# A transformer block on one Trainium2 core: the low halves of the feed-forward weights made by an adding transfer, with the sequence of all steps searched anew

## The chip, the cores and the metric

The kernel runs on one core of a Trainium2 chip. A core has five engines with an instruction queue each: PE (TensorE, matmuls), ACT (ScalarE), DVE (VectorE), POOL (GpSimd) and SP (SyncE, which here only issues transfers); 16 DMA engines move data between the core's SBUF and the chip's memory. An engine takes its instructions strictly in the order in which they were written, so an instruction that waits holds up everything behind it on its engine. The metric is the device time of one execution in microseconds (us); less is better.

## What is computed

The reference is one transformer layer in float32: S = 2048 tokens of width 640, 32 heads of width 20, an attention in which each token looks at 8 earlier tokens, two apart, and a gated feed-forward part (SwiGLU) of width 1728.

```python
def _layernorm(x, axis=-1, eps=1e-5):
    ...
B, S, D = 1, 2048, 640                         # F = 1728
def _A_ref(x, wqkv, wo):
    qkv = (x @ wqkv).reshape(B, S, 3, H, Dh)   # H = 32, Dh = 20
    ...
    off = jnp.arange(W) * dil                  # W = 8, dil = 2
    idx = pos[:, None] - off[None, :]
    ...
    logits = jnp.einsum("bhsd,bhswd->bhsw", q, kg) * scale
    logits = jnp.where(mask[None, None, :, :], logits, -1e9)
    attn = _softmax(logits, axis=-1)
    o = jnp.einsum("bhsw,bhswd->bhsd", attn, vg)
    return o.reshape(B, S, D) @ wo
def _B_ref(x, w_gate, w_up, w_down):
    g = _silu(x @ w_gate)
    u = x @ w_up
    return (g * u) @ w_down
h = x + _A_ref(_layernorm(x), A_wqkv, A_wo)
h2 = h + _B_ref(_layernorm(h), B_w_gate, B_w_up, B_w_down)
return h2
```

## The kernel before

**Numbers in halves.** TensorE multiplies here in a rounded 32-bit form (fp32r). To keep the accuracy of float32, every operand is held as two halves: the high half is the rounded value, the low half is the raw value minus the high half, rounded again. Each product is then made in three passes into the same accumulator (one PSUM bank): high times high, high times low, low times high. A high half of a weight is a copy by ACT that rounds; a low half is a subtraction by DVE (`split`, 640 columns at a time, line L956).

**Tiling.** The tokens are worked on in four blocks of 512, b = 0 to 3, and the feed-forward weights in NF = 14 column blocks, i = 0 to 13 (the last is half as wide and comes from an array of its own). Stages: layernorm and QKV projection (matmuls L643, results taken from the bank by ACT L648) for all blocks; attention on DVE, with the exponential on ACT (`att_qk` L692 and L699, `att_exp` L710 to L712, `att_av` L721 to L735, a little of it on POOL); the output projection `wo` (matmuls L890, copied out by ACT L893, added to the residual by DVE L896); a second layernorm; the feed-forward part. Between a layernorm and its matmuls the normalised tokens are turned into columns: `pair_columns` (L490 ff.) makes their halves in the tile `shb`, by ACT L495 and L506 and DVE L496 and L507. `shb` is also what the QKV matmuls read, so the columns of the first feed-forward block overwrite what the last QKV matmuls read.

**Feed-forward part.** Blocks b = 0 and b = 1 run through `ffn(b)`; b = 2 and 3 through a scheme that shares products between the two blocks. `load_ffn(b, i, ...)` brings the weights of one column block: one transfer of 960 KB of raw weights by SP (L938: 1280 columns for gate and up, 640 for down, on 128 partitions), two rounding copies by ACT (L939 with 1280 columns, L940 with 640), and three subtractions of 640 columns by DVE (L956). For b = 0 the low halves are also stored to a scratch array in memory, `lsc` (SP, L951), and b = 1 and b = 2 take them from there (L944) instead of making them. There are two raw buffers, two buffers for gate and up, three for down. Then, for column block i: three passes of five matmuls each for the gate into bank 5 and three for up into bank 6 (`proj`, L962; in the lists below bank_73 and bank_74; the others, banks 0 to 4 and 7, are bank_68 to bank_72 and bank_75); ACT takes the silu of bank 5 (`gate`, L985), which frees that bank; DVE multiplies it by bank 6 (L986), which frees bank 6; ACT rounds the product to its high half (L996), DVE makes the low half (L997); PE multiplies both with the down weights into banks 0 to 4 (`downs`, L973, three matmuls for each bank).

**What sets the order.** The program is first recorded: `P.add(engine, cost, fn, r, w, ...)` notes a step, what it reads and what it writes. `P.order()` then returns a sequence of all steps, in which each stands behind those that it depends on, and the program is written out in that sequence; so it sets the order on every engine's queue at once. Before, the sequence comes from a planner that places steps on the engines by their assumed costs in ten rounds (`listed`, `latest`), each step's planned start being moved by an entry of a table of some 300 numbers (`SHIFT`); 2846 steps are recorded. In the time that this text speaks of most, the first feed-forward block (b = 0), the attention of blocks 2 and 3, the projection `wo(1)` and its layernorm lie on DVE, ACT and PE in between.

Of the kernel before, what the change touches and what calls it, by code (L numbers as in the profile page):

```python
# [34 lines left out]
LANES, HOP = 8, 0.035  # L35
LAP = {"PE": 0.0, "ACT": 0.1, "DVE": 0.08, "POOL": 0.0, "SP": 0.0}
ROUNDS = ((1.1, 3, 3.5), (1.5, 6, 1.5), (1.4, 20, 3.5), (1.1, 6, 3.5), (1.3, 10, 3.5), (1.0, 6, 1.5), (1.0, 3, 1.5), (1.3, 3, 3.5), (1.4, 10, 2.5),)
PR = {'tp': 6, 'mx': 2, 'mh': 2, 'ml': 2, 'mld': 3, 'dt': 2.2, 'g1': 0.6, 'y1': 0.6, 'x': 0.5, 'yst': 8, 'yld': 2, 'wqd': 4, 'wqh': 0.5, 'wql': 4, 'qev': 1, 'kvs': 0.4, 'atl': 1.2, 'exp': 0.5, 'ost': 3, 'wod': 2, 'woh': 8, 'wol': 1.2, 'old': 1.5, 'fld': 4, 'lst': 6, 'wev': 1.5, 'fh': 2.2, 'fl': 8, 'ln1': 8, 't1': 1, 'wo0': 1.2, 'wo': 2.2, 'ln1t': 1.2, 'xb': 0.4, 'tr': 10, 't1t': 2.2, 'ln1d': 0.5, 'hst': 10, 'hld': 10, 'ht': 1, 'hc': 2, 'jd': 3, 'jp': 8, 'js': 4, 'jl': 0.4, 'ja': 0.5, 'jfld': 1.2, 'jfh': 4, 'jfl': 1, 'jhi': 4, 'jmu': 0.4, 'jlo': 0.9, 'jcm': 0.5, 'w3': 1, 'w3e': 8, 'w3o': 0.4, 'w3x': 8, 'w3l': 2.2, 'jy': 6}

SHIFT = {  # L40
# [34 lines left out]
}  # L75


# [1444 lines left out]
```

## Time and profile before

| what | value |
|---|---|
| time of the kernel before, three runs | 836.15 us median (835.84, 836.15, 837.64) |
| span of the profiled execution | 835.3 us |
| time of the profiled execution itself | not recorded apart from its span; the median lies 0.85 us above the span |
| PE busy | 826.3 us, 99% of the span, 4061 matmuls |
| PE weight loads (beside the matmuls) | 712.8 us, 85% |
| DVE busy | 755.7 us, 90%, 916 instructions |
| ACT busy | 421.3 us, 50%, 740 instructions |
| POOL busy | 23.1 us, 3%, 34 instructions |
| DMA | 211.08 MB moved, 253 GB/s on the mean; SP's queue 74.0% of 16 engines' span |

The page of the profile gives each engine's busy time; the views of the trace give it by stretches of time (windows), by groups of like instructions (busy us, mean ns of one, idle time before them and what ended it), by waits, and as a chain of work that ended last. Times in a trace count from the start of the span. A line number is that of the kernel's file; in the changed kernel the same lines stand 12 further down up to `load_ffn`'s rounding copies, and 18 further behind it (L962 becomes L980, L985 becomes L1003).

### The profile page before, as it was taken

Reading aid. Unit: us, or ns where it says so; the run is one execution under the profiler, and the core shown is the slowest. Engines: PE = TensorE matmul, PEld = TensorE weight load, DVE = VectorE, ACT = ScalarE, POOL = GpSimd, SP = SyncE. Lnnn points to the kernel's source line nnn. Section 1 sums busy time; section 2 is a strip of 40 time slices with the busy share of each in tenths; the row PEclk is TensorE's granted clock in tenths of the full one; section 3 lists DMA queues with packets and bytes.
Section 4 is the critical chain, followed back from the end, with each engine's and each line's share of the span. In section 5 each row is a group of like instructions: output and inputs, shape, how many; then the busy total and the mean of one; then the engine's idle time right before and its main releaser. Section 6 shows DMA issues by size and latency. Waiting matters only on the chain.

```text
span 835.3 us, 11299 instructions
## 1 busy us (share of the span) xinstructions
PE 826.3 (99%) x4061; PEld 712.8 (85%) x4061; DVE 755.7 (90%) x916; ACT 421.3 (50%) x740; POOL 23.1 (3%) x34
## 2 busy tenths in 40 slices
PE   8999999999999999999999999999999999999998
PEld 6888888889978888887888888888988888888998
DVE  7599999999999999999999999998869888777982
ACT  7856473333783435654543476565695323323440
POOL 0000000000100000001000000000000000000000
PEclk9999999999999999999999999999999999999999
DMA  8897868568679764899899758899999634457722
GB/s 274 288 348 275 267 213 283 185 207 308 186 219 343 257 197 177 326 303 349 282 313 349 271 173 315 255 288 352 352 339 320 224 115 151 124 175 258 273 99 75
DMA packets 113223, 211.08 MB, mean 253 GB/s; under 512 B 37952, under 2 KB 70400, under 8 KB 112528
## 3 DMA queue, kind: packets, MB, share of 16 engines
q1 hardware_dynamic: 112864, 209.96, 74.0%
q8 instruction: 32, 0.52, 0.2%
q10 hardware_dynamic: 304, 0.41, 0.1%
q14 instruction: 23, 0.19, 0.1%
HBM read 151.27 MB, written 59.05 MB: 252 GB/s over the span
## 4 chain that ended last, share of the span: by engine, by line
PE 84%; DVE 8%; ACT 3%; DMA 3%; issue 1%; SPq 0%; POOL 0%; DVEq 0%; ACTq 0%; POOLq 0%
PE bank L962 22%; PE bank L1046 18%; PE bank L643 15%; PE bank L973 10%; PE bank L1298 7%; PE bank L890 6%; DMA fa<-in_x_dram 2%; PE bank L1103 1%; DVE fa L692 1%; PE bank L1093 1%; DVE fa L735 1%; PE bank L1068 1%; DVE fa L727 1%; DVE fa L699 1%; ACT ra L617 1%
## 5 line engine op out<-in xcount | busy, mean ns | idle before, releaser
L962 PE MATMUL bank<-shb,ra 128*128 128x512 f32 x810 | 190.0, 390 | 1.3 <-DVE shb L507 1.3
L962 PEld LDWEIGHTS bank<-shb,ra 128*128 128x128 f32 x810 | 151.4, 188 | 32.7 <-ACT shb L506 1.5
L643 PE MATMUL bank<-ra,sha 128*128 128x480 f32 x480 | 105.2, 379 | 0.2 <-ACT ra L617 0.2
L643 PE MATMUL bank<-ra,shb 128*128 128x480 f32 x470 | 102.5, 378 | 0.0
L643 PEld LDWEIGHTS bank<-ra,sha 128*128 128x128 f32 x480 | 89.8, 188 | 14.5 <-ACT ra L617 0.6
L643 PEld LDWEIGHTS bank<-ra,shb 128*128 128x128 f32 x470 | 88.1, 188 | 13.2
L692 DVE TENSOR_TENSOR fa<-fa 128x2560 f32<-128x2560 f32 x32 | 90.2, 2820 | 0.9 <-DMA fa<-qsc 0.4
L727 DVE TENSOR_TENSOR fa<-fa 128x2560 f32<-128x2560 f32 x32 | 90.3, 2822 | 0.8
L699 DVE TENSOR_REDUCE fa<-fa 128x128 f32<-128x2560 f32 x32 | 89.9, 2810 | 0.4
L1046 PE MATMUL bank<-shb,ra 128*128 128x512 f32 x360 | 89.4, 395 | 0.6 <-DVE fa L990 0.6
L973 PE MATMUL bank<-ra,acts 128*128 128x512 f32 x328 | 80.7, 391 | 0.0
L1046 PEld LDWEIGHTS bank<-shb,ra 128*128 128x128 f32 x360 | 66.0, 188 | 16.2 <-DVE fa L1223 1.7
L735 DVE TENSOR_TENSOR fa<-fa 128x1280 f32<-128x1280 f32 (+2 forms) x70 | 76.7, 1096 | 1.3
L890 PE MATMUL bank<-ra 128*128 128x320 f32 x480 | 74.1, 310 | 0.0
L890 PEld LDWEIGHTS bank<-ra 128*128 128x128 f32 x480 | 71.7, 188 | 2.4 <-ACT fa L893 1.0
L648 ACT ACTIVATE st<-bank,fa 128x480 f32<-128x480 f32 x64 | 41.0, 656 | 64.1 <-PE bank L643 59.5
L973 PEld LDWEIGHTS bank<-ra,acts 128*128 128x128 f32 x328 | 61.1, 188 | 13.2 <-DVE acts L997 0.5
L1046 PE MATMUL bank<-ra 128*128 128x512 f32 x288 | 69.1, 390 | 0.0
L1046 PEld LDWEIGHTS bank<-ra 128*128 128x128 f32 x288 | 53.9, 188 | 11.1
L1223 DVE TENSOR_TENSOR fa<-bank,fa 128x512 f32<-128x512 f32 x60 | 41.0, 689 | 19.8 <-PE bank L1046 19.0
L939 ACT CAST ra<-fa 128x1280 fp32r<-128x1280 f32 (+1 forms) x38 | 45.6, 1207 | 22.9 <-PE bank L962 12.3
L996 ACT CAST acts<-fa 128x512 fp32r<-128x512 f32 x34 | 21.0, 620 | 48.7 <-DVE fa L986 47.0
(189 smaller groups left out, 1059.8 us busy)
## 6 DMA issues: line engine op xcount, KB each, us to landing
fa<-in_ffn_dram SPq DMA_DIRECT2D x28, 960.0 KB, 6.4
fa<-ksc SPq DMA_DIRECT2D x16, 880.0 KB, 5.4
fa<-vsc SPq DMA_DIRECT2D x16, 880.0 KB, 7.3
ra<-lsc SPq DMA_DIRECT2D x21, 640.0 KB, 5.8
ra<-lsc SPq DMA_DIRECT2D x27, 320.0 KB, 3.7
lsc<-ra SPq DMA_DIRECT2D x13, 640.0 KB, 4.6
fa<-in_ffn_dram SPq DMA_DIRECT2D x12, 640.0 KB, 4.0
ra<-tsc SPq DMA_DIRECT2D x8, 960.0 KB, 7.1
```

Of the source, the lines that this page charges most:

```text
L643: T.matmul(banks[bk][:, 0:480], l, r_(wq(g, w, c), 480), start=(p, c) == first_mm, stop=(p, c) == last_mm)
L648: P.add("ACT", act(480) + 0.06, lambda bk=bk, j=j: A.activation(stage_t()[:, so : so + 1920].rearrange("p (t j c) -> p t j c", t=3, j=NJ)[ ...
L692: P.add("DVE", dve(2560), lambda: V.tensor_tensor(f(PROD, 2560).rearrange("p (j w c) -> p j w c", j=2, w=W), window(ko, 2 * jp), f(qo + 32 ...
L699: P.add("DVE", dve(2560), lambda: V.tensor_reduce(f(lo + 128 * jp, 128), f(PROD, 2560).rearrange("p (n d) -> p n d", d=DH), axis=AX.X, op= ...
L727: V.tensor_tensor(f(PROD, 2560).rearrange("p (j w d) -> p j w d", j=2, d=DH), bass.AP(tensor=fa[:, vo : vo + 160].tensor, offset=fa[:, vo ...
L735: V.tensor_add(dst(v), v[:, :, 0:m, :], v[:, :, m : 2 * m, :])
L890: T.matmul(banks[bk][:, 0:320], l, r_(m, 320), start=p == 0 and c == 0, stop=p == 2 and c == NC - 1)
L939: P.add("ACT", act(n), lambda: A.copy(r_(gu, n), f(raw, n)), r=[rf(raw, n)], w=[rr(gu, n)], prio=PR["fh"])
L962: T.matmul(banks[bk], r_(gu + 1280 * w + wid * c + col, 128), x2(a, c), start=p == 0 and c == 0, stop=p == 2 and c == NC - 1)
L973: T.matmul(banks[bk][:, lo:hi], l, m, start=first and p == 0, stop=last and p == len(passes) - 1)
L1046: T.matmul(banks[bk], r_(ws[w] + 256 * q, 128), x(a, c), start=start and p == n == q == 0, stop=stop and p == 2 and n == len(terms) - 1 an ...
L1298: T.matmul(banks[bks[j]][:, 0:320], t(a, 128, 128 * j), r_(ws[w], 320), start=p == q == 0, stop=p == NP - 1 and q == 2)
```

## The change

In `load_ffn`, for b = 0 and the 13 full column blocks, DVE's three subtractions are gone. In their place ACT writes the negated rounded weights into the place of the low half (a multiplication by -1.0, 1280 and 640 columns), and POOL issues two transfers, of 640 KB and of 320 KB, which read the raw weights from memory again and add them onto what stands there. The store of the low halves into `lsc` and its reloading for b = 1 and 2 stay. `order()` no longer plans; it follows a table `ORDER` with the place of each of the 2859 steps.

```diff
-            split("DVE", gu + 1280, raw, gu, n, 0)
-            if last:
-                P.add("POOL", 1.0, lambda: G.memset(ra[0:64, dn[1] : dn[1] + 640].bitcast(F32), 0.0), ...)
-            split("DVE", dn[1], raw + n, dn[0], 640, 64 if last else 0)
+            if b == 0 and not last:
+                for o, at_, w in parts:
+                    P.add("ACT", act(w), lambda o=o, at_=at_, w=w: A.mul(r_(at_, w), f(raw + o, w), -1.0), r=[rf(raw + o, w)], w=[rr(at_, w)], prio=PR["fh"])
+                    P.add("POOL", 1.0, lambda o=o, at_=at_, w=w: G.dma_start(out=r_(at_, w), in_=ffn_in[i, :, o : o + w].bitcast(F32R), accum_op=ALU.add),
+                          r=[rr(at_, w)], w=[rr(at_, w)], prio=PR["fl"], nbytes=2 * nb(128, 4 * w))
+            else:
+                split("DVE", gu + 1280, raw, gu, n, 0)
+                ...
+                split("DVE", dn[1], raw + n, dn[0], 640, 64 if last else 0)
...
-SHIFT = {
-    7: 3.5, 9: -106.8, 22: 0.4, 31: -515.8, ...
+ORDER = (
+    3, 9, 10, 0, 2, 31, 6, 11, 7, 42, 15, 16, ...
...
     def order(self):
-        start = self.listed()
-        for stretch, serial, dma in ROUNDS:
-            start = self.listed(self.latest(start, stretch, dma), serial)
...
-        key = [(t + SHIFT.get(n, 0.0), n) for n, t in enumerate(start)]
...
+        place = {n: i for i, n in enumerate(ORDER)}
+        heap, out = [(place.get(n, n), n) for n in range(len(left)) if not left[n]], []
```

The number of matmuls stays at 4061 and SP's transfers at 586; DVE goes from 916 to 877 instructions, ACT from 659 to 685 beside its 32 table loads and what reads its accumulators, and POOL from 31 to 57 rows. Where the order has moved is shown at three places. A row gives the line, the operation and its tiles, and `x5` means five such instructions in a row. Of the tiles, `ra` holds weights in halves, `fa` raw values and attention, `acts` the halves of the gated product, `st` the QKV results.

**First place, the start of the first feed-forward block.** On PE before, the last QKV groups and the first feed-forward passes:

```order
L643 MATMUL bank_70<-ra,shb 128x480 x15
L643 MATMUL bank_71<-ra 128x480 x5
L643 MATMUL bank_71<-ra,shb 128x480 x5
L643 MATMUL bank_71<-ra 128x480 x5
L504 MATMUL bank_73<-fa 128x128 x2
L504 MATMUL bank_75<-fa 128x128 x4
L504 MATMUL bank_74<-fa 128x128 x4
L962 MATMUL bank_73<-shb,ra 128x512 x5
L962 MATMUL bank_74<-shb,ra 128x512 x5
L962 MATMUL bank_73<-shb,ra 128x512 x10
L962 MATMUL bank_74<-shb,ra 128x512 x10
L962 MATMUL bank_73<-shb,ra 128x512 x15
```

And after:

```order
L655 MATMUL bank_69<-ra,shb 128x480 x15
L516 MATMUL bank_75<-fa 128x128 x4
L516 MATMUL bank_74<-fa 128x128 x4
L516 MATMUL bank_73<-fa 128x128 x2
L655 MATMUL bank_68<-ra,shb 128x480 x15
L980 MATMUL bank_74<-shb,ra 128x512 x5
L980 MATMUL bank_73<-shb,ra 128x512 x5
L980 MATMUL bank_74<-shb,ra 128x512 x10
L980 MATMUL bank_73<-shb,ra 128x512 x20
L980 MATMUL bank_74<-shb,ra 128x512 x10
L980 MATMUL bank_73<-shb,ra 128x512 x5
L980 MATMUL bank_74<-shb,ra 128x512 x5
```

A QKV group into bank_68, three passes all of which read `shb`, now stands directly ahead of the feed-forward passes; before, the last QKV group went into bank_71, and its last pass reads only `ra`. On ACT before, from the last column copies to the first silu (five copies of pairs, L495, stood seven rows further up):

```order
L506 CAST shb<-bank_73 128x256
L506 CAST shb<-bank_75 128x512
L506 CAST shb<-bank_74 128x512
L939 CAST ra<-fa 128x1280
L648 ACTIVATE st<-bank_71,fa 128x3x160
L712 ACT_TABLE_LOAD
L712 ACTIVATE fa<-fa 128x256
L940 CAST ra<-fa 128x640 x2
L985 ACT_TABLE_LOAD
L985 ACTIVATE fa<-bank_73 128x512
```

And after:

```order
L507 CAST shb<-fa 128x2x128 x5
L960 ACTIVATE ra<-fa 128x1280
L660 ACTIVATE st<-bank_68,fa 128x3x160
L952 CAST ra<-fa 128x640
L724 ACT_TABLE_LOAD
L724 ACTIVATE fa<-fa 128x256
L960 ACTIVATE ra<-fa 128x640
L951 CAST ra<-fa 128x1280
L952 CAST ra<-fa 128x640
L1003 ACT_TABLE_LOAD
L1003 ACTIVATE fa<-bank_73 128x512
```

The five pair copies now stand behind the last column copies, and two of the new multiplications (L960) and one more rounding copy stand ahead of the first silu. On DVE before, up to the first gate multiplication (L986):

```order
L711 TENSOR_TENSOR fa<-fa 128x256
L956 TENSOR_TENSOR ra<-fa,ra 128x640 x2
L765 STREAM_TRANSPOSE fa<-fa 128x2x5x32 x2
L721 TENSOR_REDUCE fa<-fa 128x32
L956 TENSOR_TENSOR ra<-fa,ra 128x640
L722 RECIPROCAL fa<-fa 128x32
L723 TENSOR_TENSOR fa<-fa 128x256
L727 TENSOR_TENSOR fa<-fa 128x2560
L986 TENSOR_TENSOR fa<-bank_74,fa 128x512
```

And after, where the gate multiplication is L1004:

```order
L508 TENSOR_TENSOR shb<-fa,shb 128x2x128 x5
L733 TENSOR_REDUCE fa<-fa 128x32
L711 TENSOR_REDUCE fa<-fa 128x128
L734 RECIPROCAL fa<-fa 128x32
L735 TENSOR_TENSOR fa<-fa 128x256
L739 TENSOR_TENSOR fa<-fa 128x2560
L747 TENSOR_TENSOR fa<-fa 128x2x640
L747 TENSOR_TENSOR fa<-fa 128x2x2x160
L1004 TENSOR_TENSOR fa<-bank_74,fa 128x512
```

The subtractions are gone, and a sum over 2560 columns (L711) and two adds of the attention (L747) now stand ahead of the first gate multiplication.

**Second place, the end of `wo(1)` inside the first feed-forward block.** On PE before:

```order
L890 MATMUL bank_75<-ra 128x320 x15
L962 MATMUL bank_73<-shb,ra 128x512 x5
L962 MATMUL bank_74<-shb,ra 128x512 x5
L973 MATMUL bank_69<-ra,acts 128x512 x6
L890 MATMUL bank_75<-ra 128x320 x15
L962 MATMUL bank_74<-shb,ra 128x512 x5
L890 MATMUL bank_75<-ra 128x320 x15
L962 MATMUL bank_74<-shb,ra 128x512 x5
L962 MATMUL bank_73<-shb,ra 128x512 x15
```

And after:

```order
L902 MATMUL bank_75<-ra 128x320 x15
L980 MATMUL bank_74<-shb,ra 128x512 x5
L902 MATMUL bank_75<-ra 128x320 x15
L991 MATMUL bank_68<-ra,acts 128x512 x3
L980 MATMUL bank_74<-shb,ra 128x512 x5
L991 MATMUL bank_72<-acts,ra 128x512 x3
L991 MATMUL bank_71<-ra,acts 128x512 x3
L980 MATMUL bank_73<-shb,ra 128x512 x15
L980 MATMUL bank_74<-shb,ra 128x512 x5
L991 MATMUL bank_68<-ra,acts 128x512 x3
```

Behind the last `wo` group one group of down matmuls now stands ahead of the next pass into bank_74. On DVE before, around the gate multiplication that stands behind the last residual add (L896):

```order
L692 TENSOR_TENSOR fa<-fa 128x2560
L896 TENSOR_TENSOR h_1560<-h_1560,fa 128x640
L986 TENSOR_TENSOR fa<-bank_74,fa 128x512
L956 TENSOR_TENSOR ra<-fa,ra 128x640 x2
L997 TENSOR_TENSOR acts<-fa,acts 128x512
```

And after, where the last residual add (L908) stands in the row directly ahead of this list (gate multiplication L1004, low half of its product L1015):

```order
L1004 TENSOR_TENSOR fa<-bank_74,fa 128x512
L711 TENSOR_REDUCE fa<-fa 128x128
L733 TENSOR_REDUCE fa<-fa 128x32
L734 RECIPROCAL fa<-fa 128x32
L735 TENSOR_TENSOR fa<-fa 128x256
L469 RECIPROCAL fa<-fa 128x4
L470 TENSOR_TENSOR fa<-fa 128x4
L471 TENSOR_TENSOR fa<-fa 128x4
L472 SCALAR_TENSOR_TENSOR fa<-fa 128x4
L739 TENSOR_TENSOR fa<-fa 128x2560
L747 TENSOR_TENSOR fa<-fa 128x2x640
L1015 TENSOR_TENSOR acts<-fa,acts 128x512
```

Two subtractions stood between the gate multiplication and the low half of its product; now ten steps of attention and layernorm do.

**Third place, SP's queue in the first feed-forward blocks.** On SP before:

```order
L938 DMA fa<-in_ffn_dram 128x1920
L951 DMA lsc<-ra 128x1280
L951 DMA lsc<-ra 128x640
L678 DMA fa<-qsc 128x320
L654 DMA ksc<-st 64x2x640
```

And after:

```order
L781 DMA osc<-fa 32x5x64 x2
L969 DMA lsc<-ra 128x1280
L950 DMA fa<-in_ffn_dram 128x1920
L690 DMA fa<-qsc 128x320
L694 DMA fa<-ksc 128x1x1760
L969 DMA lsc<-ra 128x640 x2
L950 DMA fa<-in_ffn_dram 128x1920
```

The store of a low half (L969) stands directly ahead of a load of raw weights (L950). On POOL after, a stretch of the same time (before, the attention's small sums and clears stood there alone):

```order
L961 DMA ra<-in_ffn_dram 128x640
L961 DMA ra<-in_ffn_dram 128x1280
L765 TENSOR_TENSOR fa<-fa 128x1
L767 TENSOR_TENSOR fa<-fa 128x2x320
L961 DMA ra<-in_ffn_dram 128x1280
L1465 MEMSET acts 128x2
L961 DMA ra<-in_ffn_dram 128x640 x2
L961 DMA ra<-in_ffn_dram 128x1280 x2
```

The adding transfers (L961) share POOL's queue with those sums and the clear of `acts`.

More of the change, by code (lines that the diff above doesn't have):

```diff
@@ L32 @@
 SCALE = DH ** -0.5
[L35 to L37 removed]
 PR = {'tp': 6, 'mx': 2, 'mh': 2, 'ml': 2, 'mld': 3, 'dt': 2.2, 'g1': 0.6, 'y1': 0.6, 'x': 0.5, 'yst': 8, 'yld': 2, 'wqd': 4, 'wqh': 0.5, 'wql': 4, 'qev': 1, 'kvs': 0.4, 'atl': 1.2, 'exp': 0.5, 'ost': 3, 'wod': 2, 'woh': 8, 'wol': 1.2, 'old': 1.5, 'fld': 4, 'lst': 6, 'wev': 1.5, 'fh': 2.2, 'fl': 8, 'ln1': 8, 't1': 1, 'wo0': 1.2, 'wo': 2.2, 'ln1t': 1.2, 'xb': 0.4, 'tr': 10, 't1t': 2.2, 'ln1d': 0.5, 'hst': 10, 'hld': 10, 'ht': 1, 'hc': 2, 'jd': 3, 'jp': 8, 'js': 4, 'jl': 0.4, 'ja': 0.5, 'jfld': 1.2, 'jfh': 4, 'jfl': 1, 'jhi': 4, 'jmu': 0.4, 'jlo': 0.9, 'jcm': 0.5, 'w3': 1, 'w3e': 8, 'w3o': 0.4, 'w3x': 8, 'w3l': 2.2, 'jy': 6}
[L40 removed]
[34 rows of a table removed]
[L75 removed]
+ORDER = (
[143 rows of a table added]
+)
 class Plan:
@@ L102, in order @@
     def order(self):
-        start = self.listed()
-        for stretch, serial, dma in ROUNDS:
-            start = self.listed(self.latest(start, stretch, dma), serial)
-        self.start, self.end = start, max(t + o[1] for t, o in zip(start, self.ops))
-        ops = self.ops
-        left = [len(o[3]) for o in ops]
-        key = [(t + SHIFT.get(n, 0.0), n) for n, t in enumerate(start)]
-        heap, out = [key[n] for n in range(len(ops)) if not left[n]], []
+        left = [len(o[3]) for o in self.ops]
+        succ = [[] for _ in self.ops]
+        for n, o in enumerate(self.ops):
+            for d in o[3]:
+                succ[d].append(n)
+        place = {n: i for i, n in enumerate(ORDER)}
+        heap, out = [(place.get(n, n), n) for n in range(len(left)) if not left[n]], []
         heapq.heapify(heap)
@@ L114, in order @@
             out.append(n)
-            for m in self.succ[n]:
+            for m in succ[n]:
                 left[m] -= 1
                 if not left[m]:
-                    heapq.heappush(heap, key[m])
+                    heapq.heappush(heap, (place.get(m, m), m))
         return out
-    def latest(self, start, stretch, dma):
-        ops = self.ops
-        t, due = 5.0, {}
-        for n in sorted((n for n, o in enumerate(ops) if o[0] == "PE"), key=lambda n: start[n]):
-            due[n] = t
-            t += ops[n][1]
-        last = [0.0] * len(ops)
-        for n in reversed(range(len(ops))):
-            eng, cost, _, _, prio, _, nbytes = ops[n]
-            if eng == "SP":
-                cost += nbytes + dma
-            elif eng == "DVE" and prio == 20:
-                cost *= stretch
-            last[n] = min(min((last[m] - HOP for m in self.succ[n]), default=1e9) - cost, due.get(n, 1e9))
-        return last
@@ L945, in load_ffn @@
                 return
-            split("DVE", gu + 1280, raw, gu, n, 0)
-            if last:
-                P.add("POOL", 1.0, lambda: G.memset(ra[0:64, dn[1] : dn[1] + 640].bitcast(F32), 0.0), w=[rr(dn[1], 640)], prio=PR["fh"])
-            split("DVE", dn[1], raw + n, dn[0], 640, 64 if last else 0)
+            if b == 0 and not last:
[5 more added lines that the diff above has]
+                split("DVE", gu + 1280, raw, gu, n, 0)
+                if last:
+                    P.add("POOL", 1.0, lambda: G.memset(ra[0:64, dn[1] : dn[1] + 640].bitcast(F32), 0.0), w=[rr(dn[1], 640)], prio=PR["fh"])
+                split("DVE", dn[1], raw + n, dn[0], 640, 64 if last else 0)
             for o, at_, m in parts if b == 0 and i in KEPT else ():
```

75 lines of the change are left out of this document (removed), and 177 rows, old and new, of tables (ORDER, SHIFT).

## The prediction

> **What bounds the kernel now.** I read the page's totals first, then the windows of the trace, the chain of waits, and the waits themselves.
>
> ```profile
> span 835.3 us, 11299 instructions
> PE 826.3 (99%) x4061; PEld 712.8 (85%) x4061; DVE 755.7 (90%) x916; ACT 421.3 (50%) x740; POOL 23.1 (3%) x34
> core 0: us, PE busy (x) PEld busy (x) DVE busy (x) ACT busy (x) POOL busy (x), PEclk, DMA share, GB/s
> 0.00:12.00 12.00, 8.99 (x36) 6.89 (x37) 8.55 (x21) 7.87 (x19) 1.16 (x7) 1.00 0.80 270
> 12.00:231.00 219.00, 218.84 (x1051) 191.72 (x1050) 204.94 (x201) 119.43 (x241) 9.05 (x10) 1.00 0.78 258
> 231.00:252.00 21.00, 19.61 (x92) 16.20 (x91) 20.76 (x32) 16.81 (x32) 0.10 (x1) 1.00 0.70 213
> 252.00:400.00 148.00, 147.96 (x692) 124.38 (x692) 145.43 (x145) 70.80 (x111) 5.77 (x7) 1.00 0.79 277
> 400.00:560.00 160.00, 160.00 (x752) 134.69 (x751) 156.95 (x158) 86.40 (x134) 6.89 (x8) 1.00 0.84 283
> 560.00:800.00 240.00, 239.40 (x1233) 207.71 (x1232) 201.62 (x337) 113.50 (x197) 0.10 (x1) 1.00 0.70 241
> ```
>
> PE is the bound from 12 us on: its idle time is 0.16, 1.39, 0.04, 0 and 0.60 us in the five stretches from 12 to 800 us. The clock is full, so the matmuls themselves do not change. DVE runs at 98% from 252 to 400 us (145.43 of 148), the stretch of the first feed-forward block (b = 0), and PE still hardly waits: the sequence has each bank freed just in time. So an unloaded DVE has almost nothing to give here, and a sequence that is a little worse has much to lose.
>
> ```profile
> 239.66 13.90 PE bank L962 x60
> 253.56 3.40 PE bank L973 x15
> PE bank L962 <- DVE shb L507: 1.3, 1, 1.3
> SPq L951 <- DVE ra L956: 38.2, 13, 12.7
> ```
>
> The chain runs through PE; 60 matmuls take 13.90 us, so one pass of five is worth 1.13 to 1.16 (the down row: 15 in 3.40, five in 1.133, three in 0.68). The one wait of PE for the new block is 1.3 us, for the columns. SP's stores of low halves (L951) already wait 38.2 us for DVE's subtractions, at nobody's cost.
>
> **The change part by part.** *The subtractions removed, the multiplications and transfers added.*
>
> ```profile
> L956 DVE TENSOR_TENSOR ra<-fa,ra 128x640 fp32r<-128x640 f32 x40 | 31.7, 814 | 0.0
> L939 ACT CAST ra<-fa 128x1280 fp32r<-128x1280 f32 x34 | 42.7, 1263 | 21.9 <-PE bank L962 11.3 <-DMA fa<-in_ffn_dram 8.8 <-PE bank L1068 1.7
> L940 ACT CAST ra<-fa 128x640 fp32r<-128x640 f32 x32 | 23.0, 725 | 9.1 <-PE bank L973 5.6 <-issue 3.4
> fa<-in_ffn_dram SPq DMA_DIRECT2D x28, 960.0 KB, 6.4
> ra<-lsc SPq DMA_DIRECT2D x21, 640.0 KB, 5.8
> lsc<-ra SPq DMA_DIRECT2D x13, 640.0 KB, 4.6
> ```
>
> DVE loses 39 of the 40 subtractions, 39 x 0.81 = 31.7 us. None of it is on the path: PE's idle in that stretch is 0.04 us. ACT gains 13 x 1.26 + 13 x 0.73 = 25.8 us by the rows of the copies of the same shape; ACT is busy 70.80 of 148 us there, so on the mean it has room, and only the place in the queue counts. The 26 adding transfers have no row before: of one, I bound the time from issue to landing, L, below by a plain load of 640 KB (5.8 us) and above by a load and a store one after the other (5.8 + 4.6 = 10.4).
>
> *The start of the first feed-forward block.* Count from the end of the QKV group into bank_68, which now stands last. ACT in its new order: five pair copies (they overwrite `shb`, so they wait for that group), a multiplication of 1280, the QKV result, a copy of 640, the table load, the exponential. Then DVE: the sum, the 2560 sum, reciprocal, product, the 2560 product, two adds, and the gate multiplication that frees bank_74.
>
> ```profile
> 232.80 1.62 ACT L495 CAST shb<-fa 128x256 fp32r<-128x256 f32 x5
> L648 ACT ACTIVATE st<-bank,fa 128x480 f32<-128x480 f32 x64 | 41.0, 656 | 64.1 <-PE bank L643 59.5 <-issue 3.9 <-DVE fa L457 0.5
> L712 ACT ACT_TABLE_LOAD x13 | 16.7, 1283 | 0.2
> L712 ACT ACTIVATE fa<-fa 128x256 f32<-128x256 f32 x16 | 6.7, 417 | 11.1 <-DVE fa L711 11.0
> L721 DVE TENSOR_REDUCE fa<-fa 128x32 f32<-128x256 f32 x16 | 10.1, 630 | 0.0
> L699 DVE TENSOR_REDUCE fa<-fa 128x128 f32<-128x2560 f32 x32 | 89.9, 2810 | 0.4
> L722 DVE RECIPROCAL fa<-fa 128x32 f32<-128x32 f32 x16 | 5.5, 346 | 0.3
> L723 DVE TENSOR_TENSOR fa<-fa 128x256 f32<-128x256 f32 x16 | 6.7, 421 | 0.5
> L735 DVE TENSOR_TENSOR fa<-fa 128x1280 f32<-128x1280 f32 x32 | 47.5, 1485 | 0.5
> L735 DVE TENSOR_TENSOR fa<-fa 128x640 f32<-128x640 f32 x32 | 26.3, 821 | 0.6
> 246.34 2.82 DVE L727 TENSOR_TENSOR fa<-fa 128x2560 f32<-128x2560 f32 x1
> 249.08 0.68 DVE L986 TENSOR_TENSOR fa<-bank,fa 128x512 f32<-128x512 f32 x1
> ```
>
> ACT: 1.62 + 1.26 + 0.66 + 0.73 + 1.28 + 0.42 = 5.97. DVE: 0.63 + 2.81 + 0.35 + 0.42 + 2.82 + 1.49 + 0.82 + 0.68 = 10.02. Together 15.99; an instruction starts up to 0.08 before its forerunner's row is over (246.34 + 2.82 against 249.08), over the chain about 0.6, so 15.4. PE has eight passes until it needs bank_74 for the second column block (1, 1, 2, the four in a row, by the list): 8 x 1.133 = 9.1. It waits 15.4 - 9.1 = 6.3 us where 1.39 were idle in the window before: **+4.9**. Ends: +4 if instructions overlap more, +5.5 without overlap.
>
> *The end of `wo(1)`.* PE's last group of it ends; ACT copies the bank, DVE adds the residual and then multiplies the gate that frees bank_74.
>
> ```profile
> L893 ACT COPY fa<-bank 128x320 f32<-128x320 f32 x32 | 13.3, 424 | 27.5 <-PE bank L890 26.5 <-DMA fa<-qsc 0.9
> L896 DVE TENSOR_TENSOR h<-h,fa 128x640 f32<-128x640 f32 x8 | 6.4, 816 | 0.2 <-ACT fa L893 0.2
> 234.37 0.16 DVE L460 SCALAR_TENSOR_TENSOR fa<-fa 128x2 f32<-128x2 f32 x1
> L985 ACT ACTIVATE fa<-bank 128x512 f32<-128x512 f32 x34 | 20.3, 598 | 39.8 <-PE bank L962 30.2 <-DMA asc<-fa 6.3 <-PE bank L1068 1.6
> ```
>
> That is 0.42 + 0.82 + 0.68 = 1.92 against one group of three down matmuls, 0.68: **+1.2** (2.5 if a copy of 1280, 1.26, stands ahead on ACT). Right behind it the low half of that product (L1015, 0.68 like the other DVE operations on 512) stands behind ten DVE steps: 2.81 + 0.63 + 0.35 + 0.42 + 4 x 0.16 + 2.82 + 1.49 + 0.68 = 9.84, less 0.6 for overlap, 9.2. PE has five passes and two down groups, 5.67 + 1.36 = 7.0, before it needs that half: **+2.2**.
>
> *Smaller places.* By the list, in the rest of that block seven passes follow the end of the pass before in the same bank, or the down group that frees a buffer, with one group of downs or nothing in between. Each costs at least the gate multiplication, 0.68, and at most the copy of 640, the silu and the multiplication less one group, 0.73 + 0.60 + 0.68 - 0.68 = 1.33. Nearer the lower end, 0.8 each: **+5.6** (4.8 to 9.3).
>
> *SP behind the adding transfer.* The store L969 of the second column block's low half waits for its accumulation, and the raw load L950 of the fourth block stands directly behind it; that load's copy on ACT (the second of the `L951 x2`) stands ahead of the silu that frees bank_73. From the same origin: the multiplication ends at 1.62 + 1.26 = 2.9, the transfer lands L later, store and load are issued (0.6), the load takes 6.4, copy and silu 1.26 + 0.60: L + 11.8. PE gets there at 15.4 and four passes and one down group, 20.6. It waits L - 8.8: nothing at 5.8, 1.6 at 10.4. There are 13 such stores. Traffic speaks for the upper end: from 231 to 400 us the DMA engines are taken 0.70 x 21 + 0.79 x 148 = 131.6 us for 213 x 21 + 277 x 148 = 45.5 MB, 2.9 us for one MB. The raw weights read again are 13 x 960 KB = 12.8 MB: 37 us more, 168.6 of 169. I take 1.6 here and about as much in all the others: **+3** (0 to +8).
>
> The Trainium skill, "Collectives: The Full Stack", section "The bandwidth ceiling: the fold count and why AG ≠ RS ≠ AR", says that an add made by the DMA engines needs two source reads and so runs at half a copy's rate, 32.35 against 62.28 GB/s, in an exchange between cores. By that, as an estimate, a 640 KB addition is worth two loads, 11.6 us, and the place above costs 2.8 instead of 1.6. No run here shows it yet. "DMA: Bandwidth & Descriptors", section "Anatomy of one DMA — SWDGE (gpsimd) path", speaks the other way: 2.0 us plus bytes over 436 GB/s, for 640 KB an estimate of 3.5 us, by which the place costs nothing and the sum is 3 lower; but the plain load in this trace takes 5.8.
>
> *Elsewhere.* Block b = 1 and the later stages keep their steps in another order. What the trace shows to be gained there is PE's idle: 12 - 8.99 = 3.0 at the start, 0.16, 0.60. I take **-2.5**, between 0 and -3.8.
>
> Sum: 835.3 + 4.9 + 1.2 + 2.2 + 5.6 + 3 - 2.5 = 849.7. The median of the runs stands 0.85 above the span: 850.6, so **851**.
>
> **The rivals.** *The DMA engines become the bound of the first block.* If each added byte is handled twice there, 2 x 37 = 74 us come on top of 131.6: 205.6 us in a stretch of 169, 36 more than there is; half of the places above vanish inside that (7 us), so about 835.3 + 36 - 2.5 + 0.85 + 7 = 877; where large packets cost less than the mean 2.9 us per MB, 865. For it: shares of 0.70 to 0.79 already. Against: the 13 raw loads may start earlier than PE needs them, and the 160 us from 400 on hold a share of 0.84 without a wait of PE. The skill's rule of two reads, above, would bring it about.
>
> *The other side: the time falls.* DVE is the engine that frees banks and halves, at 98%. If, against my reading of the lists, PE's buffers are filled early enough that the waits above lie beside other work, unloading DVE leaves only gains: the idle of 1.39, 0.04, 0.16, 0.60 and part of the start, about 4 us: 832. It decides if the eight passes at the start are not held, that is, if the chain of 15.4 us is under 10.5. Against it: the rows add up.
>
> *The transfers are cheap.* L below 8.8: my sum without the 3, 848; with the small places at their lower end 846.
>
> **How the numbers follow.** Less than 0.2%, 1.7 us, can't be told from no change. Chances: the sum as it stands or with cheap transfers (844 to 857) 0.62; DMA engines as the bound (862 and more) 0.22; slower by less, 838 to 844, 0.05; faster 0.07; within 0.2% 0.04. So faster 0.07, same 0.04, slower 0.89. The range from 841 to 877 leaves out the faster and the unchanged case, and of the DMA case the third above 877; together about 0.2.
>
> **What would show it.** PE's waits between 231 and 400 us: one of 5 to 7 us in all at the first feed-forward passes, put down to silu and gate multiplication (L1003, L1004); 1 to 2.5 and 2 to 3 behind `wo(1)`; some of 0.7 to 1.3; DVE's idle up by some 30 us; from issue to landing 6 to 10 us for L961. It is wrong if PE stays at 99% there, if L961 lands in over 12 us (then SP's waits at L969 grow past 38 us and PE waits for L951's copies), or if PE waits after 400 us.

## The result: slower by 2.8%, nearly all of it in the first feed-forward block

The changed kernel takes 859.83 us (median of four runs, 859.52 to 860.83), the kernel before, run beside it, 836.0. The ratio is 1.0276, with a 95% interval from 1.0262 to 1.029: 23.8 us more. The forecast was 851, between 841 and 877. The profiled execution after took 860.83 us, with a span of 858.9.

The page's totals and the windows of the trace after; from 430 us on they are cut roughly where the work stands as it did in the windows of before (some 2610 of the 4061 matmuls fall before 580 us, some 2620 before 560 us in the kernel before):

```profile
span 858.9 us, 11240 instructions
PE 832.5 (97%) x4061; PEld 714.5 (83%) x4061; DVE 732.9 (85%) x877; ACT 440.1 (51%) x766; POOL 45.7 (5%) x60
core 0: us, PE busy (x) PEld busy (x) DVE busy (x) ACT busy (x) POOL busy (x), PEclk, DMA share, GB/s
0.00:12.00 12.00, 9.34 (x37) 7.42 (x38) 8.77 (x20) 7.69 (x17) 1.16 (x7) 1.00 0.84 297
12.00:231.00 219.00, 218.23 (x1053) 191.43 (x1052) 203.74 (x205) 120.70 (x250) 10.48 (x12) 1.00 0.79 256
231.00:260.00 29.00, 23.52 (x93) 18.09 (x92) 23.07 (x23) 21.09 (x31) 3.63 (x5) 0.88 1.00 294
260.00:300.00 40.00, 36.29 (x155) 28.45 (x154) 29.42 (x26) 16.13 (x20) 5.20 (x6) 1.00 0.99 285
300.00:400.00 100.00, 92.48 (x439) 77.72 (x437) 76.34 (x70) 61.36 (x97) 17.35 (x20) 0.98 0.98 277
400.00:430.00 30.00, 28.73 (x126) 23.47 (x127) 24.65 (x27) 14.99 (x22) 0.63 (x1) 1.00 0.93 314
430.00:580.00 150.00, 150.00 (x708) 126.58 (x707) 145.93 (x142) 78.95 (x126) 7.20 (x8) 1.00 0.87 300
580.00:820.00 240.00, 239.15 (x1225) 206.86 (x1224) 195.65 (x326) 106.92 (x188) 0.10 (x1) 1.00 0.69 238
```

Three things are to be read here. PE's idle time from 231 to 430 us is 5.48 + 3.71 + 7.52 + 1.27 = 18.0 us, where before it was 1.4; behind 430 us it is 0.85 us up to the last window, 0.60 before. The DMA engines, at 0.70 to 0.79 from 231 to 400 us before, stand at 0.98 to 1.00 there (the share of this view can come out a little above 1, as it does in some windows below). And the clock is below 1.00 in two windows. DVE's relief is there too, 22.8 us less busy in all, and bought nothing.

PE's timeline shows where it waited (start, duration, instructions, and in brackets the idle time ahead with its releaser; the rows without a wait and three waits of 0.46 to 0.89 us are left out):

```profile
239.35 8.68 PE L980 MATMUL bank<-shb,ra 128*128 128x512 f32 x30 [1.92 <-DVE shb L519]
250.08 4.16 PE L980 MATMUL bank<-shb,ra 128*128 128x512 f32 x10 [2.05 <-ACT fa L1003]
255.73 4.83 PE L980 MATMUL bank<-shb,ra 128*128 128x512 f32 x20 [1.50 <-DVE fa L1004]
266.33 2.58 PE L980 MATMUL bank<-shb,ra 128*128 128x512 f32 x10 [1.01 <-DMA ra<-in_ffn_dram]
292.68 3.70 PE L980 MATMUL bank<-shb,ra 128*128 128x512 f32 x15 [0.76 <-ACT ra L951]
304.99 2.57 PE L980 MATMUL bank<-shb,ra 128*128 128x512 f32 x10 [1.13 <-DVE fa L1004]
325.55 5.96 PE L980 MATMUL bank<-shb,ra 128*128 128x512 f32 x25 [0.85 <-DVE fa L1004]
370.78 1.40 PE L980 MATMUL bank<-shb,ra 128*128 128x512 f32 x5 [2.38 <-DVE fa L1004]
380.62 1.22 PE L991 MATMUL bank<-ra,acts 128*128 128x512 f32 x2 [2.33 <-DVE acts L1015]
401.27 1.43 PE L980 MATMUL bank<-shb,ra 128*128 128x512 f32 x5 [2.09 <-DMA ra<-in_ffn_dram]
```

Two waits (266 and 401 us) are for an adding transfer's landing, one (239 us) is for the columns (L519), as a wait of 1.26 us was before, and one (293 us) for a rounding copy (L951); the others are for the silu (L1003), the gate multiplication (L1004) and the low half of the product (L1015). The transfers themselves, from the queues' part of the page and the list of issues (count, size, median us to landing):

```profile
q0 software_dynamic: 3744, 12.78, 8.4%
fa<-in_ffn_dram SPq DMA_DIRECT2D x28, 960.0 KB, 7.3
ra<-in_ffn_dram POOLq DMA_DIRECT2D x13, 640.0 KB, 8.6
ra<-in_ffn_dram POOLq DMA_DIRECT2D x13, 320.0 KB, 7.9
```

An addition of 640 KB lands after 8.6 us, inside the bounds of 5.8 and 10.4. POOL's queue (q0) takes 8.4% of 858.9 us for 12.78 MB, 5.6 us of all engines per MB.

### The profile page after: what moved, and what is told of

It reads as the page before. It is cut to its first block, busy times and chain, and to the rows that moved or that the text cites. A ratio compares the mean times of both kernels' runs of the same rounds, so it can differ in the third digit from the quotient of the medians.

```text
span 858.9 us, 11240 instructions
## 1 busy us (share of the span) xinstructions
PE 832.5 (97%) x4061; PEld 714.5 (83%) x4061; DVE 732.9 (85%) x877; ACT 440.1 (51%) x766; POOL 45.7 (5%) x60
## 3 DMA queue, kind: packets, MB, share of 16 engines
q0 software_dynamic: 3744, 12.78, 8.4%
## 5 line engine op out<-in xcount | busy, mean ns | idle before, releaser
L980 PE MATMUL bank<-shb,ra 128*128 128x512 f32 x810 | 198.9, 396 | 15.6 <-DVE fa L1004 6.3
L711 DVE TENSOR_REDUCE fa<-fa 128x128 f32<-128x2560 f32 x32 | 90.0, 2811 | 0.5
L1064 PE MATMUL bank<-shb,ra 128*128 128x512 f32 x360 | 89.4, 394 | 0.7 <-DVE fa L1008 0.6
L991 PE MATMUL bank<-ra,acts 128*128 128x512 f32 x328 | 85.9, 394 | 2.3 <-DVE acts L1015 2.3
L747 DVE TENSOR_TENSOR fa<-fa 128x1280 f32<-128x1280 f32 (+2 forms) x70 | 76.9, 1098 | 2.3 <-DMA osc<-fa 0.7
L951 ACT CAST ra<-fa 128x1280 fp32r<-128x1280 f32 (+1 forms) x38 | 45.7, 1203 | 6.5 <-PE bank L980 4.1
L1223 ACT CAST ra<-fa 128x512 fp32r<-128x512 f32 x30 | 18.0, 620 | 51.3 <-PE bank L1064 27.9
```

Source lines behind the costliest of these rows:

```text
L711: P.add("DVE", dve(2560), lambda: V.tensor_reduce(f(lo + 128 * jp, 128), f(PROD, 2560).rearrange("p (n d) -> p n d", d=DH), axis=AX.X, op= ...
L747: V.tensor_add(dst(v), v[:, :, 0:m, :], v[:, :, m : 2 * m, :])
L951: P.add("ACT", act(n), lambda: A.copy(r_(gu, n), f(raw, n)), r=[rf(raw, n)], w=[rr(gu, n)], prio=PR["fh"])
L980: T.matmul(banks[bk], r_(gu + 1280 * w + wid * c + col, 128), x2(a, c), start=p == 0 and c == 0, stop=p == 2 and c == NC - 1)
L991: T.matmul(banks[bk][:, lo:hi], l, m, start=first and p == 0, stop=last and p == len(passes) - 1)
L1064: T.matmul(banks[bk], r_(ws[w] + 256 * q, 128), x(a, c), start=start and p == n == q == 0, stop=stop and p == 2 and n == len(terms) - 1 an ...
```

## The experiments

**Is it the order or the transfers?** Four runs separate the two. First, the new order with DVE's subtractions put back at the places of the transfers:

```diff
-    P.add("ACT", act(w), lambda ...: A.mul(r_(at_, w), f(raw + o, w), -1.0), ...)
-    P.add("POOL", 1.0, lambda ...: G.dma_start(out=r_(at_, w), in_=ffn_in[i, :, o : o + w].bitcast(F32R), accum_op=ALU.add), ...)
+    P.add("ACT", act(w), lambda ...: None, ...)
+    P.add("POOL", 1.0, lambda ...: V.tensor_sub(r_(at_, w), f(raw + o, w), r_(gu if o == 0 else dn[0], w).bitcast(F32)), ...)
```

> The changed kernel's order with the low halves of the first block made by DVE again, one subtraction per former adding transfer (1280 and 640 wide) at that transfer's place in the sequence; the 26 multiplications on ACT are left out. Theory A (two causes: the order holds PE for about 14 us, the transfers take another 10 by filling the DMA engines): 846 to 851 us, with the waits for silu and gate multiplication still there and the DMA share back at 0.7 to 0.8. Theory B (the transfers alone): 835 to 838. Theory C (the order alone): 857 to 862.

It took 877.58 us (ratio 1.0493, 1.0473 to 1.0513), outside all three theories, and doesn't answer the question: a subtraction at a transfer's place reads the raw buffer later than the multiplication did and holds it longer. Two subtractions waited 3.53 and 5.93 us for a raw load, so they read the next weights, and their low halves belong to the wrong column block. SP's loads L950 waited 15.6 us for these subtractions, a wait that none of the theories has.

Then the transfers kept, but cut to 16 columns, and in another run made plain copies of the full bytes:

```diff
-    G.dma_start(out=r_(at_, w), in_=ffn_in[i, :, o : o + w].bitcast(F32R), accum_op=ALU.add)
+    G.dma_start(out=r_(at_, 16), in_=ffn_in[i, :, o : o + 16].bitcast(F32R), accum_op=ALU.add)   # narrow
...
+    G.dma_start(out=r_(at_, w), in_=ffn_in[i, :, o : o + w].bitcast(F32R))                        # plain
```

> The changed kernel with every adding transfer cut to 16 columns instead of 1280 or 640, so that the low halves of the first block are not completed; order, multiplications, issues and waits for the transfers stay, their bytes go. Theory A: 846 to 850 us; landing of an adding transfer 3 to 5 us, DMA share from 231 to 400 us 0.75 to 0.8, PE's waits for L1003, L1004 and L1015 still 12 us or more. Theory B: 835 to 838, PE's waits gone. Theory C: 857 to 862.

> The changed kernel with the adding transfers made plain copies of the same bytes by the same queue, so that the low halves of the first block hold raw weights; all else stays. If an addition takes the DMA engines twice as long as a copy (5.6 us per MB in the changed kernel's queue against 2.9 for all others): the software queue's share falls from 8.4% to 4 to 5%, and the time to 850 to 855 us. If the bytes alone count, or the way in which POOL's queue is served: share and time stay, 858 to 862.

Narrow: 855.62 us (1.0232, 1.0208 to 1.0256), above the 850 at which theory A ended and just under theory C's 857. Plain: 855.82 (1.0237, 1.0214 to 1.026), 0.8 above the upper end given for an addition that takes twice as long. Most of the loss, 19.5 of 23.8 us, is there with hardly a byte moved. The windows of the narrow run, and its timeline at the start of the block:

```profile
231.00:260.00 29.00, 24.33 (x96) 18.86 (x95) 23.18 (x24) 21.39 (x32) 3.63 (x5) 0.88 0.72 221
260.00:300.00 40.00, 37.31 (x161) 29.59 (x160) 31.34 (x28) 17.03 (x20) 6.95 (x8) 1.00 0.67 227
300.00:400.00 100.00, 94.66 (x447) 79.44 (x446) 76.32 (x72) 63.01 (x99) 15.58 (x18) 0.98 0.72 226
248.64 2.57 PE L980 MATMUL bank<-shb,ra 128*128 128x512 f32 x10 [0.69 <-ACT fa L1003]
253.27 6.46 PE L980 MATMUL bank<-shb,ra 128*128 128x512 f32 x20 [2.06 <-DVE fa L1004]
```

The DMA engines are back at 0.67 to 0.72, and PE still waits for the silu and the gate multiplication; its idle time from 231 to 430 us is 12.7 us, against 18.0 with the additions. The order holds it, with the multiplications and the waits for (now small) transfers that it contains. Plain copies of all bytes cost this order 0.2 us, additions 4.2. The queues of the run with plain copies, and its issues:

```profile
q0 software_dynamic: 3744, 12.78, 5.1%
ra<-in_ffn_dram POOLq DMA_DIRECT2D x13, 640.0 KB, 6.8
```

POOL's queue takes 5.1% of a span of 853.3 us, 3.4 us per MB, so an addition keeps the engines 1.66 times as long as a copy by the same queue.

Last of the four, the old order with multiplication and addition where the subtractions stood:

```diff
+            if b == 0 and not last:
+                def low(o, at_, w):
+                    A.mul(r_(at_, w), f(raw + o, w), -1.0)
+                    G.dma_start(out=r_(at_, w), in_=ffn_in[i, :, o : o + w].bitcast(F32R), accum_op=ALU.add)
+                for o, at_, w, fn_ in ((0, gu + 1280, 640, lambda: low(0, gu + 1280, 1280)), (640, gu + 1920, 640, lambda: None), (1280, dn[1], 640, lambda: low(1280, dn[1], 640))):
...
```

The first of the three places now holds the work for 1280 columns, the second nothing, the third that for 640.

> The kernel before, its order of all steps kept, with the multiplication and the adding transfer written where DVE's subtractions stood. Theory A: 842 to 852 us: the DMA engines at 0.95 or more in the first feed-forward block and the multiplications somewhere in ACT's way, but none of the holds that the new order has. Theory B: 855 to 865, as much as the change. Theory C: 835 to 838.

885.05 us (1.0575, 1.0558 to 1.0593), worse than any theory had it. The waits of PE and of SP's queue in it (its L971, L994 and L953 are L962, L985 and L951 of before; columns: us in total, times, longest):

```profile
PE bank L971 <- DMA ra<-in_ffn_dram: 13.6, 8, 3.6
PE bank L971 <- ACT fa L994: 10.1, 3, 8.1
SPq L953 <- DMA ra<-in_ffn_dram: 106.9, 18, 16.8
```

Here the landing of the additions costs most: the stores of low halves wait 106.9 us for them (38.2 for the subtractions before, 48.8 for the additions in the changed kernel) with raw loads behind them, and PE waits 13.6 us for additions, 3.1 in the changed kernel. With the same transfers the old order takes 25 us more than the new one, so the new one does place them better.

**Two limits beside each other.** If the order alone costs 19.5 us, another order should save that, unless the transfers hold it. The first feed-forward block was sequenced again, by the durations and landing times of the changed kernel's trace:

```diff
 ORDER = (
...
-    427, 422, 1014, 976, 1015, 423, 638, 628, ...
+    422, 423, 976, 420, 421, 632, 1014, 624, ...
...
```

> The changed kernel with its 26 multiplications and 26 adding transfers unaltered; only the sequence of the steps in the first feed-forward block is another (places 698 to 1315 of the table), arranged by the durations and landing times that the changed kernel's trace shows, so that silu and gate multiplication stand ahead of copies and attention steps that nobody awaits. Theory A (the order holds PE, the transfers can be hidden): 833 to 840 us, PE's waits in that block under 3 us although the DMA share stays at 0.95 or more. Theory B (adding transfers at 0.98 of the DMA engines hold PE whatever the order): 848 to 860.

860.74 us (1.0278, 1.0261 to 1.0296): not a microsecond won. But the trace is another one (the lines stand 4 further down; the second half shows rows of ACT's and PE's timelines and of the waits):

```profile
231.00:260.00 29.00, 28.51 (x131) 22.99 (x129) 25.90 (x26) 20.39 (x32) 2.72 (x4) 1.00 0.98 288
260.00:300.00 40.00, 35.12 (x146) 28.06 (x145) 30.74 (x28) 20.89 (x25) 8.66 (x10) 0.96 1.01 317
259.78 1.26 ACT L955 CAST ra<-fa 128x1280 fp32r<-128x1280 f32 x1 [7.89 <-DMA fa<-in_ffn_dram]
263.79 0.51 PE L995 MATMUL bank<-ra,acts 128*128 128x512 f32 x1 [3.48 <-ACT acts L1018]
PE bank L984 <- ACT ra L955: 3.6, 5, 1.2
ACT ra L955 <- DMA fa<-in_ffn_dram: 18.8, 7, 7.9
PE bank L984 <- DMA ra<-in_ffn_dram: 2.7, 2, 2.1
```

The start of the block is mended (idle 0.49 us from 231 to 260, where it was 5.48), and then the DMA engines are full and the waits have moved: PE waits for copies (L955) that wait 18.8 us for raw weights, for additions that have not landed, and, longest of all, 3.48 us for the high half of a product (L1018), which on ACT stands behind a copy that waited 7.89 us for raw weights. The same order, with the transfers made narrow and made plain, by the same edits as above:

> The re-sequenced first feed-forward block with every adding transfer cut to 16 columns, so that the low halves of that block are not completed. Theory D (two limits lie beside each other, each enough for some 20 us: the changed kernel's order, which costs 19 us even with narrow transfers, and the load of the DMA engines, which the re-sequenced block ran into): 836 to 843 us, DMA share about 0.75, PE's waits in the block under 4 us. Theory E (the re-sequenced block is another order with holds of its own, the bytes matter as little as in the changed order, 4 us): 852 to 858.

> The re-sequenced first feed-forward block with plain copies of the full bytes in place of the additions, so that its low halves hold raw weights. With narrow transfers this order takes 838.6 us, with full additions 860.7. If it is the addition's double handling (5.6 us of a DMA engine per MB against 3.4 for a copy by the same queue) that fills the engines: 839 to 848 us, DMA share near 0.9. If the 12.8 MB as such hold this order: 852 to 860.

Narrow: 838.63 us (1.0024, 1.0014 to 1.0035). Plain: 845.5 (1.0101, 1.0083 to 1.0119). In the narrow run:

```profile
231.00:260.00 29.00, 28.54 (x131) 23.09 (x130) 26.27 (x26) 23.05 (x34) 4.45 (x6) 1.00 0.82 267
260.00:300.00 40.00, 40.00 (x178) 33.14 (x177) 38.09 (x34) 22.06 (x28) 7.51 (x9) 1.00 0.89 292
300.00:400.00 100.00, 97.86 (x469) 82.52 (x469) 87.77 (x81) 63.19 (x100) 15.17 (x18) 1.00 0.72 231
```

Both lie in the ranges that their expectations gave for two limits and for the addition's double handling. Put side by side (us, medians; beside these runs the kernel before took 836.0 to 837.6), this is the answer:

| order of the first block | narrow | plain copies | additions |
|---|---|---|---|
| as changed | 855.62 | 855.82 | 859.83 |
| sequenced again | 838.63 | 845.50 | 860.74 |

In the upper row the order is the limit, and its waits leave the DMA engines time to move nearly everything for nothing. Take those waits away, and the transfers are the limit: 22 us between narrow and additions, 7 for the bytes and 15 for the addition. Along that lower row the share of the DMA engines from 260 to 300 us goes from 0.89 to 1.01 and 1.01, and the median landing of POOL's transfers from 5.1 (8 KB each) to 6.3 and 8.4 us (640 KB each); the runs don't separate full engines from later landings. The multiplications on ACT are in all six; with them and without DVE's subtractions the narrow run still lies 2 us above before, so in this order what DVE was relieved of brought nothing.

**Can an order spread the transfers?** All steps of the changed kernel, and all of the kernel before, were sequenced again twice: by one trace's landing times, and then with each transfer queued behind those issued ahead of it, additions at twice their bytes, with margins. The edit is a new `ORDER` throughout (in the kernel before it takes the planner's place):

```diff
-        order = P.order()
+        order = ORDER
```

> As the run with the first feed-forward block in another sequence, but all steps of the kernel re-sequenced in the same way. Theory A: 830 to 836 us, below the kernel before by what PE's idle at the start gives (3 us at most) and a little of the 1.9 us wait at the first feed-forward block. Theory B: 845 to 860.

> The kernel before, with DVE's subtractions and without any adding transfer, re-sequenced in the same way. If what a new sequence gives has nothing to do with the change: 831 to 835 us, the same as or below the fully re-sequenced changed kernel. If DVE's 31.7 us are worth something once the order uses them: 836, and the re-sequenced changed kernel lies 2 us or more below it.

> The changed kernel with full adding transfers, all steps in another sequence again, arranged this time with every transfer queued behind the ones issued before it (an adding transfer counted with twice its bytes) and with margins on landing and hops, instead of with the landing times of one trace. Theory D (order and DMA load are two separate limits, and an order can spread the load): 836 to 848 us, DMA share under 0.95 in the first feed-forward block. If adding transfers cost 15 us or more in any order: 852 or more.

> The kernel before, without adding transfers, re-sequenced in the same way as the other run of this call. If the sequence alone can win what PE's idle time in the kernel before shows (3.0 us at the start, 1.4, 0.6, 0.2): 831 to 835 us, and it lies below the re-sequenced changed kernel by what the transfers cost. If the sequence of before is at its end: 836 to 840.

By one trace's landing times: 908.22 us with the change (1.0872, 1.0834 to 1.0909) and 881.06 without (1.0519, 1.0493 to 1.0546). Both missed the nearest of their forecasts by 45 us and more, with and without the additions. That landing times of one trace don't fit another order is the likely reason, but it isn't shown alone: the second pair has a queue and margins at once. With these: 854.65 with the change (1.0216, 1.0182 to 1.0251; single runs from 850.9 to 862.6), 836.12 without (0.9993, 0.9979 to 1.0006). The former came out as its second branch said (852 or more), 5 us below the changed kernel, and its DMA engines are full:

```profile
231.00:260.00 29.00, 25.86 (x116) 20.24 (x115) 25.61 (x30) 20.32 (x33) 5.36 (x7) 1.00 1.04 341
300.00:400.00 100.00, 97.06 (x463) 82.65 (x462) 78.06 (x69) 62.09 (x98) 17.12 (x19) 0.98 0.98 283
```

So with full additions no order tried here has a median below 854, and without them this way of sequencing won nothing that can be told from noise. No version beat the kernel before. Whether an order exists that carries the full additions near 836 stays open.

**Does the slow clock cost anything?** In the changed kernel the granted clock falls after three of the waits. Four of the longest waits, these three among them, were filled with matmuls into a bank that nobody reads:

```diff
+        FILL = {420: (7, 9600), 1088: (15, 9600), 1106: (13, 14400), 1325: (10, 12160)}
         for n in order:
             P.ops[n][2]()
+            if n in FILL:
+                fill(*FILL[n])      # k times T.matmul(banks[7], r_(o, 128), r_(o, 512), ...)
```

> The changed kernel with idle PE filled at four of its longest waits: 7, 15, 13 and 10 matmuls of 512 columns on weights that are there already, into bank 7, which nobody reads then (45 matmuls, 10 us of PE, added in time in which it waits). In the changed kernel the granted clock falls to 0.50 for 3.3 us after a wait of about 2 us, three times. If that costs time: clock 1.00 between 236 and 256 and near 382 us, 855 to 858 us. If the loss lies within waits for ACT and DVE: clock 1.00, time 858.5 to 861, the waits longer by what the matmuls are shorter. If fillers delay the real passes: 861 to 864.

859.71 us (1.0273, 1.0252 to 1.0293). Windows of the changed kernel, and then of the run with fillers, with the row of PE that starts after the third filled wait:

```profile
240.00:245.00 5.00, 5.00 (x17) 3.93 (x16) 0.88 (x3) 2.54 (x4) 0.90 (x1) 0.66 1.02 298
250.00:255.00 5.00, 4.16 (x10) 2.77 (x10) 4.93 (x4) 1.81 (x3) 2.01 (x4) 0.66 1.01 364
```

```profile
240.00:245.00 5.00, 5.00 (x24) 4.14 (x23) 1.39 (x5) 3.76 (x6) 0.90 (x1) 1.00 1.06 359
250.00:255.00 5.00, 5.00 (x24) 4.14 (x23) 4.92 (x4) 1.10 (x2) 2.58 (x4) 1.00 1.01 333
255.64 4.70 PE L980 MATMUL bank<-shb,ra 128*128 128x512 f32 x20
```

The clock is full there and the time the same. At the start of the block, where two of the falls were, the passes behind the third wait begin at 255.64 us with fillers and at 255.73 without: the slow matmuls lay within the wait for ACT and DVE. The clock fell once all the same, after a wait of 2.76 us that ends at 371.86 us, which was not filled (0.50 from 372 to 374 us); behind the later wait for an addition both runs go on together, at 401.29 and 401.27 us. The run with plain copies says the same without fillers: at its start the clock stayed full, and PE went on at 253.33 us, as in the narrow run (253.27), where it fell twice.

## Why the prediction was right, and where its sum was not

The sign, the place and the main mechanism held: PE waits in the first block for silu and gate multiplication that stand behind work nobody awaits. The narrow run and the re-sequenced narrow run show it, since with the same steps and hardly a byte the order alone decides between 855.62 and 838.63. The sum gave 14.4 us over the span and 23.6 were measured. The time lies in the gap between the two cases that had most of the chances, the sum (844 to 857) and full DMA engines (862 and more); it is in the range because the range spans both. By its terms:

- **The start, +4.9.** The chain of 15.4 us was right as far as the order goes: in the narrow run PE goes on at 253.27, 15.9 us after the QKV group (237.4 in both runs). In the changed kernel it is 255.73, 18.3 us, because one row of it was not a duration but a wait:

```profile
243.26 0.73 ACT L952 CAST ra<-fa 128x640 fp32r<-128x640 f32 x1 [2.44 <-DMA fa<-in_ffn_dram]
245.75 0.64 DVE L733 TENSOR_REDUCE fa<-fa 128x32 f32<-128x256 f32 x1 [4.87 <-ACT fa L724]
```

  The copy of 640 waits 2.44 us for raw weights, and the exponential and DVE's attention stand behind it. The narrow run issues that load at the same time (233.94 against 234.00 us) and has no wait there, so the full additions delayed it. From 237.4 to 255.73 PE has the same 9.1 us of passes, so 9.2 us are lost (5.5 idle, the rest matmuls at a low clock), less 1.39: 7.8, not 4.9.
- **The end of `wo(1)`, +1.2, and the low half, +2.2.** Measured 2.38 and 2.33. The first came out at the upper end that was given: ACT's copy of the bank stood behind two operations of 1280 columns.

```profile
366.45 1.25 ACT L951 CAST ra<-fa 128x1280 fp32r<-128x1280 f32 x1
367.60 1.27 ACT L960 ACTIVATE ra<-fa 128x1280 fp32r<-128x1280 f32 x1
368.77 0.40 ACT L905 COPY fa<-bank 128x320 f32<-128x320 f32 x1
369.20 0.83 DVE L908 TENSOR_TENSOR h<-h,fa 128x640 f32<-128x640 f32 x1 [3.22 <-ACT fa L905]
369.94 0.68 DVE L1004 TENSOR_TENSOR fa<-bank,fa 128x512 f32<-128x512 f32 x1
```

- **Seven small places, +5.6.** Six are seen, 0.46 to 1.13 us each, 4.7 together, five for the silu or the gate multiplication and one for a copy; the size per place was right.
- **The landing, +3.** The size came out by luck. The term was worked out from SP's chain (store, raw load, copy, silu), which by its own formula costs nothing at the measured L of 8.6, under 8.8. What PE waited for was the landing itself, directly: 1.01 and 2.09, 3.1 together, a wait that the sum didn't have. (The second ends just past the 400 us behind which PE was not to wait; it is still inside the block, whose work runs some 20 us later than before.) With the late raw load above, and by the run with narrow transfers (4.2), the additions cost this order somewhat more. SP's stores (L969) waited 48.8 us for additions, past the 38 that the prediction named as a sign of being wrong, though an addition of 640 KB landed after 8.6 us in the median, not over 12.
- **Elsewhere, -2.5.** This term failed. PE's idle in the first 12 us went from 3.0 to 2.7, and in the next window from 0.2 to 0.8; behind 430 us nothing came. That an order is written anew gives no reason to count its gains where it has nothing to mend.

Of the 23.6 us, 17.4 are idle time of PE and 6.2 its busy time, 832.5 against 826.3. The latter are for the most part matmuls at a low clock, three times 3.4 us at half speed, which the start's 7.8 hold in part; the run with fillers shows that at the start they lie within the waits.

The rival of the DMA engines was weighed as an alternative to the order. It was no alternative: it stands right beside it, 22 us high as soon as the order's waits are gone. Its sum, 36 us too much for a stretch of 169, is borne out by no run: in the old order the same transfers cost 49 us, but there the engines' share was 0.88 from 300 to 400 us and PE waited for landings, so they weren't full throughout. The Trainium skill, "Collectives: The Full Stack", section "The bandwidth ceiling: the fold count and why AG ≠ RS ≠ AR", has an addition at half of a copy's rate in an exchange between cores; here it holds the engines 1.66 times as long (5.6 against 3.4 us per MB) and lands after 8.6 us against 6.8, so the direction holds and the factor is smaller. The prediction's estimate of 3.5 us for a transfer of this size, from the Trainium skill, "DMA: Bandwidth & Descriptors", section "Anatomy of one DMA — SWDGE (gpsimd) path", did not hold in this traffic even for plain copies (6.8).

The rival on the other side, a gain of 4 us from the unloaded DVE, fell in the orders tried: with the order mended and the bytes gone, the kernel still stands 2 us above before.

## What to carry to other kernels

When a profile shows one engine at 99% and hardly a wait, expect little from work taken off another engine (here nothing was won), and ask whether what replaces it finds room in every queue it passes. Test order and traffic against each other in a table of two by two: each alone can hide the other, and mending one then looks useless. Be wary of landing times read from the trace of another order: here both full sequences built on them were the slowest of their kind, and those that counted the queue's load, with margins, were 45 to 54 us faster.

## What the hardware showed beyond that

After three waits of PE (1.92, 2.05 and 2.33 us) the granted clock of TensorE fell to 0.50 for some 3.4 us; after two others of 2.38 and 2.09 us it did not. At the same place, after the same wait, it fell in the narrow run (1.91 us; 30 matmuls took 8.67 us) and not in the run with plain copies (1.90 us; 7.09). The Trainium skill, "TensorE: Matmul & The Clock Gate", section "Part 1: The HAM clock gate (the "warmup" mystery)", has two states, half and full clock, decided over a free-running window of about 3.4 us. The 0.50 and the 3.4 us agree with that; why a wait shorter than such a window is sometimes enough and sometimes not, these traces don't show. In the run with fillers the clock stayed at 1.00 at all four places, fell once elsewhere, and the time did not move.
